# Values' products on four parts of 32 columns in place of two of 64, and the first pair turned and hashed whole

## The chip, the core and the metric

The kernel runs on one core of one Trainium2 chip. Five engines work side by side: TensorE (PE in the profile, its weight loads PEld), VectorE (DVE), ScalarE (ACT), GpSimd (POOL) and SyncE (SP), which here only issues DMAs. Each engine runs its own instructions in order and waits for others by semaphores. The metric is the device time of one execution, in microseconds.

## The reference

Attention over hash buckets, and behind it a feed-forward layer. Everything is float32.

```python
batch, n_heads, seq, head_dim = (4, 8, 768, 64)        # proj: 64 x 6
q_bits = (np.einsum('bhsd,dk->bhsk', q, proj) > 0)     # k_bits likewise
q_bucket = np.sum(q_bits * 2 ** np.arange(n_bits), axis=-1)
mask = q_bucket[:, :, :, None] == k_bucket[:, :, None, :]
scores = np.where(mask, np.matmul(q, k.transpose(0, 1, 3, 2)) / np.sqrt(D), -1000000000.0)
attn = np.exp(scores - np.max(scores, axis=-1, keepdims=True))
attn = attn / (np.sum(attn, axis=-1, keepdims=True) + 1e-09)
attn_out = np.matmul(attn, v)
x = attn_out.transpose(0, 2, 1, 3).reshape(3072, 512)
h = x @ w_in                                           # 512 x 2048
out = (h / (1.0 + np.exp(-1.702 * h))) @ w_out         # 2048 x 512
```

## The kernel before, in words

The attention stage takes two heads of one batch at a time: 16 pairs, `n` from 0 to 15. The two heads (index `j`) lie one above the other on the 128 partitions, 64 rows each, with the head's 64 dimensions as rows once keys and queries are turned. A sequence of 768 is six key tiles of 128 (`kt` or `t`), and two query halves of 384 columns (`c`, `HS` = 384).

Per pair TensorE does the following.

- `scores(n, c, kts)`, L426: for each key tile, two bf16 products that compare the hash bits (`kf`, `qf`) and two f32 products of keys and queries (`kT`, `qT`), one per head, into one PSUM tile `ps`. ScalarE takes the exponential of it into `es[c]` (L436). Three PSUM tiles of tag "s" take turns.
- `values(n, c, kts)`, L453: for each key tile and head the product of the head's values with the exponentials. The 64 value columns of a head are the weights, so the two heads' products write rows 0 to 63 and 64 to 127 of one PSUM tile `av`. A 385th column carries a tiny constant. `unload` (L474) lets ScalarE write the result to `xT`.
- `hashed(n)`, L405: four products, each with 32 weight columns, of projections with keys and queries; `featured` (L414) has VectorE make bits of them and DMAs bring the bits to `kf` and `qf`.
- `total(n)`, L480: four products, each with 32 weight columns of ones, which sum the exponentials (`dn`). VectorE inverts them (`invert`) and scales the result (`norm`, L507).

An f32 product is executed in two passes, each with a weight load of its own, so every f32 product stands in the profile as two loads and two matmuls.

GpSimd adds up the first three exponentials of a half (`add_low`, L443 and L444) and VectorE the rest (`add_high`, L449 and L451). VectorE also turns later pairs' keys and queries by 32 x 32 blocks (`turn`, L394) and converts one chunk of `w_in` per pair from float64, in which the weights come, to float32 (`convert`, L158).

For pairs 1 to 15 the order on TensorE is scores of half 0, scores of half 1, values of half 0, values of half 1, hash of pair n+2 (up to n = 13), sums of pair n. The order of instructions on TensorE, VectorE, ScalarE and GpSimd is that of the program text, since the schedule is set by hand for these four (`ORDERED`, L18). SP is not among them: its DMAs are placed by what they depend on. So a DMA that must not go early is held by a small VectorE memset of its destination, which stands at the right place in VectorE's order (`behind`, L315; `late`, L162).

The first pair has a path of its own, `first_pair`, L344. Keys and queries come in plain layout and are turned by TensorE with an identity (`turned`, L366: six f32 products for one half of one operand, moved out of PSUM by VectorE or ScalarE); `bits`, L374, hashes one half and makes its bits. Before the change, the first half of keys and of queries is turned and hashed ahead of the scores, then the second half of the keys is turned; the other three steps are returned as functions (`rest`) and called between the scores of the first pair (L534 to L543). The pair's values are fetched from inside `first_pair` (L364), behind a VectorE memset (L338).

The feed-forward stage follows on TensorE without a break: first products at L727 (a Strassen scheme of seven products with sums on VectorE and GpSimd), then second products at L839.

Of the kernel before, what the change touches and what calls it, by code (L numbers as in the profile page):

```python
# [38 lines left out]
def kernel(  # L39
# [17 lines left out]
    nc = tc.nc  # L57

    loader = [nc.sync]
    B, H, S, D = q.shape  # L60
# [3 lines left out]
    T = S // P  # L64
# [90 lines left out]
        later.append((m, x))  # L155
        masks[x] = m.to_broadcast([P, CW])

    def convert(cv, dst, src, queue=None, psum=None, late=False):  # L158


        raw = cv.tile([P, CW, 2], U32, tag="raw", name="raw")
        if late:  # L162
            nc.vector.memset(raw[:, 0, 0:1], 0)
        (queue or loader[0]).dma_start(out=raw, in_=src)

        def of(x):
            return x if len(dst.shape) == 2 else x.rearrange("p (x r) -> p x r", r=dst.shape[2])

        lo, hi = raw[:, :, 0], raw[:, :, 1]
        bits = cv.tile([P, CW], U32, tag="bits", name="bits")  # L170
        if psum is None:
            part, size = dst.bitcast(U32), hi.bitcast(F32)
        else:
            part = psum.tile([P, CW], U32, tag="part", name="part")
            size = psum.tile([P, CW], F32, tag="size", name="size")
        yield


        if psum is None:
            nc.vector.scalar_tensor_tensor(part, hi, 3, masks[0x3FFFFFFF], op0=Alu.logical_shift_left, op1=Alu.bitwise_and)  # L180
        else:
            nc.vector.tensor_scalar(part, hi, 3, 0x3FFFFFFF, op0=Alu.logical_shift_left, op1=Alu.bitwise_and)
        yield
        nc.vector.scalar_tensor_tensor(bits, hi, 0xC0000000, part, op0=Alu.bitwise_and, op1=Alu.bitwise_or)
        yield

        if psum is None:
            nc.vector.tensor_tensor(part, bits, masks[0xFF800000], op=Alu.bitwise_and)
        else:
            nc.vector.tensor_scalar(part, bits, 0xFF800000, None, op0=Alu.bitwise_and)  # L190

        nc.scalar.activation(size, hi.bitcast(F32), Act.Square)
        part = part.bitcast(F32)
        yield
        nc.vector.scalar_tensor_tensor(part, lo, 2.0**-52, part, op0=Alu.mult, op1=Alu.mult)
        yield
        nc.vector.tensor_tensor(dst, of(bits.bitcast(F32)), of(part), op=Alu.add)
        yield

        nc.vector.scalar_tensor_tensor(dst, of(size), (1.125 * 2.0**-15) ** 2, dst, op0=Alu.is_ge, op1=Alu.mult)  # L200
# [3 lines left out]
    in_chunks = [(w_in_sb[:, kc, f : f + CW], wi[kc, :, f : f + CW])  # L204
                 for f0 in range(0, FF // 2, CW) for f in (f0, FF // 2 + f0) for kc in range(KC)]
# [79 lines left out]
    def attention(ff):  # L285
# [4 lines left out]
        with actx:  # L290
            ld = actx.enter_context(tc.tile_pool(name="ld", bufs=1))
            wk = actx.enter_context(tc.tile_pool(name="wk", bufs=2))
            cv = actx.enter_context(tc.tile_pool(name="cv", bufs=1))
# [8 lines left out]
            es = [ep.tile([P, T, 2, HS + 1], F32, name=f"e{i}") for i in range(2)]  # L302
# [12 lines left out]
            def behind(x):  # L315

                nc.vector.memset(x, 0.0)
# [14 lines left out]
            def fetch_v(n):  # L332
                b, hp = pairs[n]
                x = ld.tile([P, T, 2, D], F32, tag="v", name="v", bufs=2)
                if n == 0:
                    x = x.rearrange("p t j d -> p (t j d)").rearrange("p (j t d) -> p t j d", j=2, d=D)
                vts[n] = x
                if n <= 1:  # L338
                    behind(x[:, 0, :, 0])
                for j in range(2):  # L340
                    order = "(t p) d -> p t d" if n else "(p t) d -> p t d"
                    loader[0].dma_start(out=x[:, :, j, :], in_=v[b, 2 * hp + j].rearrange(order, p=P))

            def first_pair():  # L344


                b, hp = pairs[0]
                x = {}
                for i, (name, src) in enumerate((("k", k), ("q", q))):
                    raw = raws[0, name] = ld.tile([P, S // 32, 32], F32, tag=name, name=name)  # L350
                    x[name] = raw.rearrange("p s i -> p (s i)").rearrange("p (j t d) -> p j t d", j=2, d=D)
                    for j, queue in enumerate((nc.sync, nc.scalar)):
                        queue.dma_start(out=x[name][:, j], in_=src[b, 2 * hp + j].rearrange("(p t) d -> p t d", p=P))
                    if i == 0:
                        for j, queue in enumerate((nc.sync, nc.scalar)):
                            queue.dma_start(out=pj[D * j : D * (j + 1)], in_=proj)
                    xts[0, name] = wk.tile([P, S], F32, tag=f"{name}T", name=f"{name}T")

                nc.scalar.activation(const.tile([1, 1], F32, name="first"), ones[0:1, 0:1], Act.Exp)
                for _ in range(4):  # L360
                    nc.tensor.matmul(aps.tile([P, 512], F32, tag="av", name="warm"), idle[:, 0:P], idle, start=True, stop=True)
                hash_weights()

                fetch_v(0)  # L364

                def turned(name, c, move):  # L366
                    tp = sps.tile([P, 2, 512], F32, tag="s", name="tp")[:, 0, 0:HS]
                    for i in range(GT):
                        for j in range(2):
                            nc.tensor.matmul(tp[D * j : D * (j + 1), i * P : (i + 1) * P], x[name][:, j, c * GT + i, :], ident,  # L370
                                             start=True, stop=True)
                    move(xts[0, name][:, c * HS : (c + 1) * HS], tp)

                def bits(name, c):  # L374
                    cols = slice(c * HS, (c + 1) * HS)
                    h = sps.tile([P, 2, 512], F32, tag="s", name="hash0")[:, 0, 0:HS]
                    nc.tensor.matmul(h, pf0[name].rearrange("p j d -> p (j d)"), xts[0, name][:, cols], start=True, stop=True)  # L377
                    nc.vector.tensor_scalar(feats[0][name][:, cols], h, above0[name][:, 0:1], FEAT[name],
                                            op0=Alu.is_gt, op1=Alu.mult)

                measure(0, "k")
                turned("k", 0, nc.vector.tensor_copy)
                turned("q", 0, nc.scalar.copy)
                measure(0, "q")
                bits("k", 0)
                bits("q", 0)
                turned("k", 1, nc.vector.tensor_copy)

                return (lambda: bits("k", 1), lambda: turned("q", 1, nc.vector.tensor_copy), lambda: bits("q", 1))

            def turn(n, name):
                x = raws[n, name]
# [3 lines left out]
            def measure(n, name):  # L396

                x = raws[n, name]
                i = 2 * n + "kq".index(name)
                junk = st.tile([P, S], BF16, tag="junk", name="junk", bufs=1)  # L400
                nc.scalar.activation(junk, x.rearrange("p s i -> p (s i)"), Act.Square, accum_out=sizes[:, i : i + 1])
# [51 lines left out]
            def values(n, c, kts):  # L453
                if 0 in kts:


                    if c and n == 0 or c and n + 2 > last:
                        avs[n, c] = mps.tile([P, HS + 1], F32, tag="m", name="av")
                    elif c:
                        avs[n, c] = sps.tile([P, 2, 512], F32, tag="s", name="av1")[:, 0, 0 : HS + 1]  # L460
                    else:
                        avs[n, c] = aps.tile([P, HS + 1], F32, tag="av", name="av")
                av, vt = avs[n, c], vts[n]
                for t in kts:
                    for j in range(2):
                        nc.tensor.matmul(av[D * j : D * (j + 1), :], vt[:, t, j, :], es[c][:, t, j, :],  # L466
                                         start=(t == 0), stop=(t == T - 1))

            def x_of(n):
                b, hp = pairs[n]  # L470
# [39 lines left out]
            conv = {}  # L510
# [4 lines left out]

            def begin(n):
                if 0 <= n - 2 < len(in_chunks) - LATE:
                    conv[n] = convert(cv, *in_chunks[n - 2], late=n == 2)
                    step(n)


# [10 lines left out]

            low, high, every = range(GT), range(GT, T), range(T)
            rest = first_pair()  # L534
            for x in "kq":
                fetch(1, x)
            scores(0, 0, low[:2])
            rest[0]()
            scores(0, 0, low[2:])
            rest[1]()  # L540
            add_low(0, 0)
            scores(0, 0, high)
            rest[2]()  # L543
            turn(1, "k")
            measure(1, "k")
            values(0, 0, low)
# [17 lines left out]
            for n in range(1, last + 1):  # L564
# [44 lines left out]
                if n < last:  # L609
                    begin(n + 1)  # L610
# [429 lines left out]
```

## Time and profile before

| what | value |
|---|---|
| runs before | 872.75 us median of 3 (872.38 to 874.32) |
| the profiled execution | 872.38 us, span 870.6 us |
| granted TensorE clock, mean | 0.997 |
| TensorE busy | 860.3 us, 99% of the span |
| VectorE, ScalarE, GpSimd busy | 719.4, 312.8, 313.3 us |
| attention on TensorE | up to 319.2 us, then first products to 607.7, second products to the end |
| one pair in the steady part | 19.14 us |
| values' products (L466) | 768 passes, 128.2 us busy |
| hash (L411) and sums (L487) | 15 and 16 blocks of eight passes |

In lines of the profile, "128*64 128x385" is a product with 128 rows and 64 columns of weights that writes or streams 385 columns. A row with "x48" merges 48 instructions: its first number is the start of the first, its second the busy time. Matmuls run on in a pipeline and their ends are modelled; starts are the better measure. The chain of work that ended last lists pieces of one engine's work, each with its share of the path. In a view by stretches, an engine's busy time stands with its instruction count in brackets, in the order TensorE, weight loads, VectorE, ScalarE, GpSimd, then the granted clock, the DMA share and GB/s.

### The profile page before, as it was taken

Reading aid. Unit: us, or ns where it says so; the run is one execution under the profiler, and the core shown is the slowest. Engines: PE = TensorE matmul, PEld = TensorE weight load, DVE = VectorE, ACT = ScalarE, POOL = GpSimd, SP = SyncE. Lnnn points to the kernel's source line nnn. Section 1 sums busy time; section 2 is a strip of 40 time slices with the busy share of each in tenths; the row PEclk is TensorE's granted clock in tenths of the full one; section 3 lists DMA queues with packets and bytes.
Section 4 is the critical chain, followed back from the end, with each engine's and each line's share of the span. In section 5 each row is a group of like instructions: output and inputs, shape, how many; then the busy total and the mean of one; then the engine's idle time right before and its main releaser. Section 6 shows DMA issues by size and latency. Waiting matters only on the chain.

```text
span 870.6 us, 11943 instructions
## 1 busy us (share of the span) xinstructions
PE 860.3 (99%) x4077; PEld 502.3 (58%) x4077; DVE 719.4 (83%) x1023; ACT 312.8 (36%) x518; POOL 313.3 (36%) x275
## 2 busy tenths in 40 slices
PE   9999999999999999999999999999999999999996
PEld 4444444444444444444444444444888888888885
DVE  4589999999999887778777778888888977897786
ACT  4866667777666643322233222332000000000000
POOL 4243223323323466665543344659903100000000
PEclk9999999999999999999999999999999999999998
DMA  4536654445763204555455555575844685468524
GB/s 103 92 56 128 108 90 84 84 85 111 108 95 68 61 3 171 189 208 198 174 195 181 206 181 204 183 253 179 299 164 157 199 245 198 162 212 242 193 97 99
DMA packets 169156, 132.00 MB, mean 152 GB/s; under 512 B 123616, under 2 KB 138112, under 8 KB 163712
## 3 DMA queue, kind: packets, MB, share of 16 engines
q1 hardware_dynamic: 166528, 129.70, 52.3%
q10 hardware_dynamic: 2560, 1.46, 0.7%
q8 instruction: 34, 0.56, 0.3%
q14 instruction: 34, 0.28, 0.1%
HBM read 79.69 MB, written 50.33 MB: 149 GB/s over the span
## 4 chain that ended last, share of the span: by engine, by line
PE 95%; DVE 3%; DMA 0%; issue 0%; SPq 0%; ACTq 0%; ACT 0%; DVEq 0%
PE product L727 33%; PE product L839 26%; PE ps L435 18%; PE av L466 15%; PE hash L411 1%; PE dn L487 1%; DVE y L819 1%; DVE xT L843 1%; DMA q<-in_q_dram 0%; PE hash L377 0%; DVE t_x L843 0%; PE tp L370 0%; DVE t2a L223 0%; DVE raw_g L222 0%; DVE v L843 0%
## 5 line engine op out<-in xcount | busy, mean ns | idle before, releaser
L436 ACT ACTIVATE e<-ps 128x768 f32<-128x768 f32 x192 | 151.2, 812 | 29.6 <-PE ps L435 27.0
L435 PE MATMUL ps<-qT,kT 64*128 64x384 f32 x768 | 155.1, 482 | 0.0
L727 PE MATMUL product<-xT,w_in_sb 128*128 128x512 f32 x288 | 135.5, 593 | 0.0
L466 PE MATMUL av<-e,v 128*64 128x385 f32 x768 | 128.2, 488 | 0.0
L443 POOL TENSOR_TENSOR acc<-e 128x768 f32<-128x768 f32 x32 | 51.1, 1597 | 196.8 <-ACT e L436 165.2
L735 ACT ACTIVATE c<-c 128x512 f32<-128x512 f32 x72 | 45.3, 630 | 186.8 <-issue 78.6
L466 PEld LDWEIGHTS av<-e,v 128*64 128x64 f32 x768 | 54.1, 136 | 71.6 <-issue 69.7
L727 PEld LDWEIGHTS product<-xT,w_in_sb 128*128 128x128 f32 x288 | 54.7, 190 | 69.0 <-issue 64.4
L727 PE MATMUL product<-t_x,s_in 128*128 128x512 f32 x192 | 90.2, 592 | 0.0
L435 PEld LDWEIGHTS ps<-qT,kT 64*128 64x128 f32 x768 | 68.0, 188 | 38.3 <-issue 38.2
L221 POOL TENSOR_TENSOR v<-c,u 128x512 f32<-128x512 f32 x24 | 34.2, 1423 | 122.4 <-ACT c L735 122.4
L852 ACT COPY u<-product 128x256 f32<-128x256 f32 x21 | 7.8, 372 | 172.1 <-PE product L839 138.9
L727 PEld LDWEIGHTS product<-t_x,s_in 128*128 128x128 f32 x192 | 36.5, 190 | 45.9 <-issue 43.2
L435 PE MATMUL ps<-qf,kf 64*128 64x384 bf16 x384 | 62.8, 324 | 0.0
L444 POOL TENSOR_TENSOR acc<-acc,e 128x768 f32<-128x768 f32 x32 | 56.4, 1763 | 2.7 <-ACT e L436 0.3
L449 DVE SCALAR_TENSOR_TENSOR acc<-e 128x768 f32<-128x768 f32 x32 | 46.0, 1438 | 4.0 <-ACT e L436 4.0
L727 PE MATMUL product<-xT,s_in 128*128 128x512 f32 x96 | 45.1, 592 | 0.0
L727 PE MATMUL product<-t_x,w_in_sb 128*128 128x512 f32 x96 | 45.1, 592 | 0.0
L435 PEld LDWEIGHTS <-kf 64*128 64x128 bf16 x384 | 18.9, 94 | 34.7 <-issue 5.7
L451 DVE TENSOR_TENSOR acc<-acc,e 128x768 f32<-128x768 f32 x32 | 35.6, 1112 | 3.7 <-DVE acc L449 0.5
L451 DVE TENSOR_TENSOR acc<-acc,acc 128x768 f32<-128x768 f32 x32 | 31.2, 974 | 6.7 <-POOL acc L444 3.1
L839 PE MATMUL product<-raw_g,xT 128*128 128x256 f32 x152 | 35.1, 379 | 0.0
(209 smaller groups left out, 1495.6 us busy)
## 6 DMA issues: line engine op xcount, KB each, us to landing
raw_g<-g_dram SPq DMA_DIRECT2D x22, 1024.0 KB
s_in<-g_dram SPq DMA_DIRECT2D x20, 1024.0 KB
g_dram<-c SPq DMA_DIRECT2D x72, 256.0 KB
g_dram<-t SPq DMA_DIRECT2D x48, 256.0 KB
raw<-in_moe_w_in_dram SPq DMA_DIRECT2D x16, 512.0 KB
raw<-in_moe_w_out_dram SPq DMA_DIRECT2D x16, 512.0 KB
v<-in_v_dram SPq DMA_DIRECT2D x32, 192.0 KB
g_dram<-u SPq DMA_DIRECT2D x24, 256.0 KB
```

Source lines behind the costliest of these rows:

```text
L221: return [lambda: eng.tensor_tensor(t1, b12, b11, op=Alu.subtract), lambda: eng.tensor_tensor(b12, b22, b12, op=Alu.subtract), lambda: eng ...
L411: nc.tensor.matmul(h[r0 : r0 + 32, :], pf[x], xts[n, x][:, c * HS : (c + 1) * HS], start=True, stop=True)
L435: nc.tensor.matmul(ps[:, j, 0:HS], a[hs, keys], m[hs, cols], start=not last, stop=last)
L436: nc.scalar.activation(es[c][:, kt, :, 0:HS], ps[:, :, 0:HS], Act.Exp, scale=1.0 / D**0.5)
L443: nc.gpsimd.tensor_tensor(acc, es[c][:, 0, :, 0:HS], es[c][:, 1, :, 0:HS], op=Alu.add)
L444: nc.gpsimd.tensor_tensor(acc, acc, es[c][:, 2, :, 0:HS], op=Alu.add)
L449: nc.vector.scalar_tensor_tensor(acc, e[0], T * TINY, e[1], op0=Alu.add, op1=Alu.add)
L451: nc.vector.tensor_tensor(acc, acc, x, op=Alu.add)
L466: nc.tensor.matmul(av[D * j : D * (j + 1), :], vt[:, t, j, :], es[c][:, t, j, :], start=(t == 0), stop=(t == T - 1))
L727: nc.tensor.matmul(ps, wq[LEFT[i]][:, kc, :], xq[RIGHT[i]][:, kc, :], start=(kc == 0), stop=(kc == K2 - 1))
L735: nc.scalar.activation(c, c, Act.Gelu_apprx_sigmoid)
L839: nc.tensor.matmul(ps, wq[LEFT[i]][:, c, :], gq[RIGHT[i]][:, c, :], start=(c == 0), stop=(c == F4 - 1))
```

## The change

There are two parts.

First, `values` splits the 64 value columns of each head into two parts of 32. Each key tile has four products of 32 weight columns (two per head, with the same exponentials streamed by both), in place of two of 64. They write the four quarters of the same PSUM tile `av`.

Second, the start of the first pair is put in another order. Both halves of the keys, then both halves of the queries are turned ahead of any hash. ScalarE moves both halves of the queries out of PSUM, VectorE both of the keys. Three of the four hashes are done ahead of the scores and the last one between the scores of key tiles 0 to 2 and 3 to 5. The pair's values are fetched after `first_pair`, without the memset that held them, so SP issues them directly behind the first queries. The memset that held the first chunk of `w_in` is gone as well (`late`): on SP that chunk's DMA now stands right behind the first pair's values, ahead of pair 1's keys and queries; before, it stood behind pair 3's bits.

```diff
-    def convert(cv, dst, src, queue=None, psum=None, late=False):
+    def convert(cv, dst, src, queue=None, psum=None):
...
-        if late:
-            nc.vector.memset(raw[:, 0, 0:1], 0)
         (queue or loader[0]).dma_start(out=raw, in_=src)
...
                 vts[n] = x
-                if n <= 1:
+                if n == 1:
                     behind(x[:, 0, :, 0])
...
                 hash_weights()
-                fetch_v(0)
...
                 measure(0, "k")
                 turned("k", 0, nc.vector.tensor_copy)
+                turned("k", 1, nc.vector.tensor_copy)
                 turned("q", 0, nc.scalar.copy)
+                turned("q", 1, nc.scalar.copy)
                 measure(0, "q")
                 bits("k", 0)
                 bits("q", 0)
-                turned("k", 1, nc.vector.tensor_copy)
-                return (lambda: bits("k", 1), lambda: turned("q", 1, nc.vector.tensor_copy), lambda: bits("q", 1))
+                bits("k", 1)
+                return lambda: bits("q", 1)
...
                     for j in range(2):
-                        nc.tensor.matmul(av[D * j : D * (j + 1), :], vt[:, t, j, :], es[c][:, t, j, :],
-                                         start=(t == 0), stop=(t == T - 1))
+                        for d in range(0, D, 32):
+                            nc.tensor.matmul(av[D * j + d : D * j + d + 32, :], vt[:, t, j, d : d + 32], es[c][:, t, j, :],
+                                             start=(t == 0), stop=(t == T - 1))
...
-                    conv[n] = convert(cv, *in_chunks[n - 2], late=n == 2)
+                    conv[n] = convert(cv, *in_chunks[n - 2])
...
             rest = first_pair()
+            fetch_v(0)
             for x in "kq":
                 fetch(1, x)
-            scores(0, 0, low[:2])
-            rest[0]()
-            scores(0, 0, low[2:])
-            rest[1]()
+            scores(0, 0, low)
+            rest()
             add_low(0, 0)
             scores(0, 0, high)
-            rest[2]()
```

## The prediction

> **What bounds the kernel now.** I read the page first (busy time per engine), then the chain that ended last around one pair of the attention stage, then TensorE and its weight loads at a seam between two kinds of products, then the first 20 us.
>
> ```profile
> PE 860.3 (99%) x4077; PEld 502.3 (58%) x4077; DVE 719.4 (83%) x1023; ACT 312.8 (36%) x518; POOL 313.3 (36%) x275
> PE 95%; DVE 3%; DMA 0%; issue 0%; SPq 0%; ACTq 0%; ACT 0%; DVEq 0%
> ```
>
> TensorE is busy for 99% of the span and 95% of the chain. So only what changes the length of TensorE's own sequence counts, and any change of it counts in full. The chain by pieces, two pairs of attention:
>
> ```profile
> 100.49 7.92 PE av L466 x48
> 108.41 0.78 PE hash L411 x8
> 109.19 0.65 PE dn L487 x8
> 109.84 9.80 PE ps L435 x72
> 119.63 7.92 PE av L466 x48
> 127.55 0.78 PE hash L411 x8
> 128.33 0.65 PE dn L487 x8
> ```
>
> A pair takes 19.14 us (119.63 less 100.49). The hash and the sums (dn) are the same work: four f32 products of 128 rows by 32 columns over 384 columns of data, each in two hardware passes, hence x8. But dn takes 0.65 and the hash before it 0.78. The reader is to see those 0.13 us: the hash follows the values' products, which lie on 64 columns, while dn follows products that already lie on 32. TensorE and its loads there:
>
> ```profile
> 126.41 1.15 PE L466 MATMUL av<-e,v 128*64 128x385 f32 x6
> 127.48 0.52 PE L411 MATMUL hash<-kT,pf_k 128*32 128x384 f32 x2
> 127.49 0.52 PE L411 MATMUL hash<-qT,pf_q 128*32 128x384 f32 x2
> 127.83 0.49 PE L411 MATMUL hash<-kT,pf_k 128*32 128x384 f32 x2
> 127.84 0.49 PE L411 MATMUL hash<-qT,pf_q 128*32 128x384 f32 x2
> 128.15 0.83 PE L487 MATMUL dn<-acc,ones 128*32 128x384 f32 x8
> ```
> ```profile
> 119.56 0.20 PEld L466 LDWEIGHTS av<-e,v 128*64 128x64 f32 x4 [0.54 <-issue]
> 119.94 0.14 PEld L466 LDWEIGHTS av<-e,v 128*64 128x64 f32 x2 [0.18 <-issue]
> 120.26 0.14 PEld L466 LDWEIGHTS av<-e,v 128*64 128x64 f32 x2 [0.18 <-issue]
> 120.59 0.14 PEld L466 LDWEIGHTS av<-e,v 128*64 128x64 f32 x2 [0.18 <-issue]
> 127.83 0.13 PEld L487 LDWEIGHTS dn<-acc,ones 128*32 128x32 f32 x4 [0.19 <-issue]
> ```
>
> In the values' block two products run side by side, and a new round of passes starts every 0.323 us (the loads at 119.94, 120.26, 120.59). In hash and dn four run side by side, all within 0.02 us of each other, and the round after starts 0.32 later (127.83 to 128.15). dn's weights were loaded at 127.83, during the hash: no gap at a seam of 32 to 32.
>
> **The change part by part.**
>
> *Rounds of the values.* 384 products of 64 columns become 768 of 32, so 768 passes become 1536. A key tile still needs two rounds, now of four. Cost per round by the nearest row: dn, two rounds in 0.65, against 24 rounds in 7.92 less the seam, 0.323. Zero, over 384 rounds. The cover is that all four columns' worth run at once; without it a key tile takes four rounds, 384 x 0.323 = 124 us more, and the hash and dn rows speak against that. Bounds: 0 below (the rounds stream the same 385 columns), and above 0.014 a round, because the starts of four parts are spread by 0.01 to 0.02 (127.48 to 127.49) and that spread might add up when rounds follow one another for 8 us, which no row shows. I take zero, as in dn. Issue: a round needs 8 instructions (4 loads, 4 passes) in 0.323, 40 ns each; the turning of keys at 8.97 issues 24 in 0.63, 26 ns each.
>
> The Trainium skill, in "TensorEngine Tiling (Array Packing)", Instruction Overhead, gives each matmul an overhead of about 60 cycles and so warns against splitting what is small. At the 2.4 GHz of "TensorE: Matmul & The Clock Gate" that is an estimate of 25 ns, and paid in line by 768 added passes 19 us; by that the forecast would be near 888. The dn rows show no such payment between four parts side by side, so the sum here does without it.
>
> *Seams.* After the values come the hash (14 times, at 24.19 and at 13 places from 50.92 to 280.6) or dn (the last two pairs). All 16 seams become 32 to 32 and lose 0.13: 16 x 0.13 = 2.1 us less. Also the first round of a values' block lasts 0.38 (119.56 to 119.94) against 0.35 in the hash (127.48 to 127.83), whose loads are shorter: 0.03 for each of 18 blocks (15 pairs with one, the first pair with three), 0.5 us less. Bounds: 0 (the waits below) and 2.6; I take 2.6, since both rows stand next to the place. Would something else hold the hash or dn then? The hash waits for VectorE's turns, which end at 121.5, 6 us ahead; dn waits for the acc that ends at 126.0, 2.1 us ahead. What is late next is VectorE itself, which looks full:
>
> ```profile
> 100.00:148.00 48.00, 48.00 (x340) 22.09 (x336) 45.61 (x57) 31.75 (x53) 16.12 (x10) 1.00 0.63 111
> ```
>
> 45.61 of 48 us. But its norm (L507) takes 1.96 there, overlapping a GpSimd sum that follows the exponentials and so TensorE, and takes 1.08 at 287.90. So 0.88 us a pair is give, and 0.16 is asked for.
>
> *The start.* Before and after do the same turns and hashes; their order differs.
>
> ```profile
> 3.68 1.64 PE L370 MATMUL tp<-ident,k 128*64 128x128 f32 x12
> 5.62 1.71 PE L370 MATMUL tp<-ident,q 128*64 128x128 f32 x12 [0.30 <-DMA q<-in_q_dram]
> 8.97 0.88 PE L370 MATMUL tp<-ident,k 128*64 128x128 f32 x12
> 11.54 0.91 PE L377 MATMUL hash<-kT,pf_k 128*128 128x384 f32 x2
> ```
>
> Before, scores begin at 9.82 and values at 17.48, with one hash, one turn and one hash between the six scores. After: keys' first turn from 3.65, and the second behind it (1.64 and 1.71 at the slow early pace, some 0.4 of it the last pass running out, so about 1.28 each in a sequence) until 6.2, which fills the 0.30 wait for the queries (landed 5.6). Queries' turns at 6.2 and 7.5, the second partly at the fast pace, until about 8.4. Three hashes of 0.65 from 8.5 to 10.5; the queries' bits are ready on VectorE at about 10.5 (hash done 9.9, 0.62 to write). Scores from 10.6: three at 0.81 to 13.0, the last hash with a seam on each side to 13.9, three more to 16.4. That is 1.1 us before 17.48. It has fewer seams, and nothing to wait for in the exponentials (ScalarE takes 0.81 each, three buffers).
>
> The values' load leaves its place behind VectorE's copy (5.98) and is issued at about 2.4, and the first chunk of w_in, which no VectorE memset holds any longer, goes right behind it on SP: 0.39 and 0.52 MB, beside the queries and ahead of pair 1's keys and queries. The chunk waits only for the first keys (3.6), so SP is not held for long. Worst case for the queries: all of the values ahead of them, 0.39 MB at the 250 GB/s that the busiest microseconds of the start moved at least (264 from 7 to 8 us, 301 from 4 to 5), 1.6 us, so turns from 7.2 rather than 6.2, and the gain falls to 0.1. For pair 1: keys and queries can be issued at about 6.3 and 9 where they were at 9.93 and 14.26, because their buffers come free sooner, and are wanted by VectorE at 18.12 and 21.98; 0.9 MB ahead costs 3.6 us at the same rate, so they land hardly later than before, and well before they are wanted. Bounds of the start: 1.3 gained (turns at the fast pace), 0.3 lost (queries late and slow pace longer). I take 0.8 gained, nearer the laid-out sequence than the worst case. The removed memsets (0.06 each on VectorE) count nothing; VectorE waits there 2.0 us for TensorE anyway.
>
> **Sum.** 2.6 + 0.8 = 3.4 us less. The profiled execution took 872.38 (span 870.6 and 1.8 around it), so 869.0; the median of the runs stands 0.37 above it, so 869.3. What follows attention is TensorE's chain without a gap (the product L727 takes 288.60 in one piece), so the gain is carried to the end.
>
> **The rivals.** (a) Longer rounds, the slower case: four parts in a long series cost more than two. 384 rounds; it turns the forecast at 3.4/384 = 9 ns a round. At the 14 ns above: 5.4 more, 874.7; at 20 ns 877. For it: no row has more than four such rounds in a series. Against: hash into dn keeps 0.32. (b) The start gains nothing or loses up to 0.3: 870.1 to 870.4. For it: 0.9 MB moved early beside the queries. Against: the second key turn covers the queries' wait. (c) The seams are saved but another engine holds the pair at 19.14 (VectorE's row above): only the start is left, 872.0. Against: the 0.88 us of give.
>
> **Numbers.** Forecast 0.56, (b) 0.14, (c) 0.13, (a) 0.17. A measurement of this kernel tells about 0.2%, 1.75 us, so faster is below 871.0 and slower above 874.5. Faster: forecast and nearly all of (b), 0.68. Same: (c) and the near end of (a), 0.16. Slower: 0.16. Range 867.6 (both terms at their best, 3.9, and the spread of the runs) to 873.6, which leaves out (a).
>
> **What would show it.** Right: av blocks near 7.9 with passes 128*32, the hash piece 0.65, a pair near 18.98, values first at about 16.4 to 16.9. Wrong: rounds above 0.33; the hash still 0.78; a wait before dn or scores on VectorE; values' first start after 17.5; queries landing after 6.5.

## The result, and the profile after

| | before | after |
|---|---|---|
| median | 872.67 us (six runs, 872.38 to 874.32) | 869.84 us (six runs, 869.47 to 871.11) |
| ratio of the times | | 0.9967, 95% interval 0.9954 to 0.9980 |
| the profiled execution | 872.38 us, span 870.6 | 869.86 us, span 868.1 |
| granted TensorE clock, mean | 0.997 | 0.996 |

The change is faster by 2.8 us by the medians and by 2.5 us by the two profiled executions. The forecast was 869.3. The page of the changed kernel, its busy times and its chain:

```profile
PE 857.6 (99%) x4845; PEld 499.7 (58%) x4845; DVE 719.2 (83%) x1020; ACT 313.4 (36%) x519; POOL 313.6 (36%) x275
PE 97%; DVE 2%; DMA 0%; issue 0%; ACTq 0%; ACT 0%; DVEq 0%
```

TensorE issues 768 passes more (4845 for 4077) and is busy 2.7 us less. So the split has not been paid for in rounds. The chain around one steady pair (start, length, what):

```profile
99.78 7.90 PE av L465 x96
107.68 0.65 PE hash L408 x8
108.33 0.65 PE dn L486 x8
108.97 9.79 PE ps L432 x72
118.77 7.90 PE av L465 x96
126.67 0.65 PE hash L408 x8
127.32 0.64 PE dn L486 x8
```

The pair takes 18.99 us (118.77 less 99.78). The hash has gone from 0.78 to 0.65, the values from 7.92 to 7.90 with twice the passes. TensorE at the seam (start, busy time, what):

```profile
118.70 7.97 PE L465 MATMUL av<-e,v 128*32 128x385 f32 x96
126.49 0.49 PE L408 MATMUL hash<-kT,pf_k 128*32 128x384 f32 x2
126.51 0.49 PE L408 MATMUL hash<-qT,pf_q 128*32 128x384 f32 x2
126.81 0.49 PE L408 MATMUL hash<-kT,pf_k 128*32 128x384 f32 x2
126.83 0.49 PE L408 MATMUL hash<-qT,pf_q 128*32 128x384 f32 x2
127.13 0.83 PE L486 MATMUL dn<-acc,ones 128*32 128x384 f32 x8
```

By starts, 24 rounds and the seam take 7.79 us (118.70 to 126.49), where before they took 7.92 (119.56 to 127.48). The weight loads of the same block:

```profile
118.70 0.16 PEld L465 LDWEIGHTS av<-e,v 128*32 128x32 f32 x8 [0.54 <-issue]
119.05 0.13 PEld L465 LDWEIGHTS av<-e,v 128*32 128x32 f32 x4 [0.19 <-issue]
119.37 0.13 PEld L465 LDWEIGHTS av<-e,v 128*32 128x32 f32 x4 [0.19 <-issue]
```

The first round lasts 0.35 (118.70 to 119.05), which was 0.38, and each one after it 0.32, with four loads where there were two. VectorE in the same stretch of 48 us as before (columns: TensorE, loads, VectorE, ScalarE, GpSimd, clock, DMA share, GB/s):

```profile
100.00:148.00 48.00, 48.00 (x490) 22.00 (x484) 45.59 (x57) 31.07 (x53) 16.06 (x10) 1.00 0.67 110
```

TensorE is still busy for all of it, so VectorE, at 45.59, does not hold the shorter pair. The start on TensorE (start, busy time, what, and in brackets the idle time before it):

```profile
4.04 2.90 PE L366 MATMUL tp<-ident,k 128*64 128x128 f32 x24 [0.32 <-DMA k<-in_k_dram]
6.64 2.61 PE L366 MATMUL tp<-ident,q 128*64 128x128 f32 x24
9.18 0.91 PE L373 MATMUL hash<-kT,pf_k 128*128 128x384 f32 x2
...
11.52 0.34 PE L432 MATMUL ps<-qf,kf 64*128 64x384 bf16 x2
...
17.42 2.15 PE L465 MATMUL av<-e,v 128*32 128x385 f32 x24
```

Here the change has brought next to nothing: the values begin at 17.42, and began at 17.48. The queries landed at 6.60 and 7.06 (5.58 and 5.75 before), their turns end at about 9.2, and the scores begin at 11.52.

An execution can be cut into three pieces by starts on TensorE: until the values first start, from there to the first product of the feed-forward layer, and the rest. This table, from the traces of all the kernels of this study, is the main tool of what follows; e1 to e11 are the experiments below.

| kernel | profiled execution | values first | from there to feed-forward | one steady pair | the rest |
|---|---|---|---|---|---|
| before | 872.38 | 17.48 | 301.74 | 19.140 | 553.16 |
| after | 869.86 | 17.42 | 299.29 | 18.990 | 553.15 |
| e1 split alone | 871.61 | 18.77 | 299.54 | 18.990 | 553.30 |
| e2 start alone | 871.08 | 16.14 | 301.74 | 19.140 | 553.20 |
| e3 64, then 32 | 873.92 | 18.84 | 301.85 | 19.140 | 553.23 |
| e4 32, then 64 | 874.43 | 17.40 | 303.82 | 19.278 | 553.21 |
| e5 after again | 870.33 | 17.84 | 299.29 | 18.990 | 553.20 |
| e6 loads held | 870.30 | 17.17 | 299.71 | 18.990 | 553.42 |
| e7 close warm-up | 869.82 | 17.20 | 299.29 | 18.990 | 553.33 |
| e8 close warm-up, loads held | 868.80 | 15.88 | 299.72 | 18.990 | 553.20 |
| e9 old order, close warm-up | 871.04 | 18.61 | 299.29 | 18.990 | 553.14 |
| e10 new order, close warm-up | 868.90 | 15.91 | 299.72 | 18.990 | 553.27 |
| e11 no warm-up | 869.71 | 17.19 | 299.29 | 18.990 | 553.23 |

The rest is the profiled execution's time less the values' first start and the piece behind it; it stays within 0.28 us over all thirteen. So nearly all that tells these executions apart lies in these two pieces. Between before and after, the attention stage gives 2.45 us and the start 0.06.

### The profile page after: what moved, and what is told of

It is laid out like the page before. It is cut to its first block, busy times and chain, and to the rows that moved or that the text cites. A ratio compares the mean times of both kernels' runs of the same rounds, so it can differ in the third digit from the quotient of the medians.

```text
span 868.1 us, 13473 instructions
## 1 busy us (share of the span) xinstructions
PE 857.6 (99%) x4845; PEld 499.7 (58%) x4845; DVE 719.2 (83%) x1020; ACT 313.4 (36%) x519; POOL 313.6 (36%) x275
## 4 chain that ended last, share of the span: by engine, by line
PE 97%; DVE 2%; DMA 0%; issue 0%; ACTq 0%; ACT 0%; DVEq 0%
PE product L724 33%; PE product L836 27%; PE ps L432 18%; PE av L465 15%; PE dn L486 1%; PE hash L408 1%; DVE xT L840 1%; PE tp L366 1%; DVE y L816 1%; DMA k<-in_k_dram 0%; PE hash L373 0%; DVE v L840 0%; DVE t2a L221 0%; DVE raw_g L220 0%; ACTq L823 0%
## 5 line engine op out<-in xcount | busy, mean ns | idle before, releaser
L465 PE MATMUL av<-e,v 128*32 128x385 f32 x1536 | 128.0, 487 | 0.0
L465 PEld LDWEIGHTS av<-e,v 128*32 128x32 f32 x1536 | 48.6, 109 | 76.2 <-issue 73.8
```

What stands on the lines that cost most here:

```text
L465: nc.tensor.matmul(av[D * j + d : D * j + d + 32, :], vt[:, t, j, d : d + 32], es[c][:, t, j, :], start=(t == 0), stop=(t == T - 1))
```

## The experiments

### The parts one at a time, and the seams: e1 to e4

The theory: the seams give their 2.5 us wherever the values stand at 32 columns next to hash or dn, and rounds of four parts cost nothing. The rival: the saving has another source (shorter passes, or the start). e1 is the kernel before with the split alone, e2 the changed kernel without the split, and e3 and e4 are the kernel before with one query half split:

```diff
                     for j in range(2):
-                        nc.tensor.matmul(av[D * j : D * (j + 1), :], vt[:, t, j, :], es[c][:, t, j, :],
-                                         start=(t == 0), stop=(t == T - 1))
+                        w = 32                       # e1;  e3: w = 32 if c else 64;  e4: w = 64 if c else 32
+                        for d in range(0, D, w):
+                            nc.tensor.matmul(av[D * j + d : D * j + d + w, :], vt[:, t, j, d : d + w], es[c][:, t, j, :],
+                                             start=(t == 0), stop=(t == T - 1))
```

> The kernel before with the split into four parts of 32 alone. My theory: all of what the pairs gain comes from the split, through the seams: values to the first product of the feed-forward stage 2.4 to 2.5 us shorter than before, a pair 19.00 in place of 19.14, the start as before (values first at 17.4 to 17.6). Time about 870.2, ratio 0.997. Rival (the reordered start and the early loads carry part of it): less than 1.5 us, over 871.

> The kernel after with the two products of 64 put back, so that only the order of the start and the early loads are new. My theory: a pair takes 19.14 again, hash 0.78; the start is worth what the profile after shows, 0.06 earlier, so the time is that of before within 0.5 us (872.2 to 873.2). Rival, the prediction's own term: 0.8 us less, 871.9. Rival, the early loads do harm later in the stage: over 873.5.

> The kernel before, with values of half 0 on two parts of 64 and of half 1 on four of 32. Seam theory: the change of width only moves from the end of the values to their middle, so values and hash together last as before within 0.05 (8.59 a pair from the first value to dn's start) and a pair 19.12 to 19.15; the hash itself 0.65. Rival, that rounds of 32 columns are themselves shorter or load better: half of the gain stays, a pair near 19.07.

> The kernel before, with values of half 0 on four parts of 32 and of half 1 on two of 64: as many products as the run beside it, in the other order, so one width change more (32 to 64 in the middle, 64 to 32 at the hash). Seam theory: a pair 0.10 to 0.15 longer than before, 19.24 to 19.29. Rival, rounds of 32 are shorter: a pair near 19.07, as in the run beside it.

Measured: e1 871.48 us (median of 12), ratio 0.9983 with the interval 0.9973 to 0.9993; e2 871.23 (of 11), 0.9984, 0.9975 to 0.9992; the kernel before beside them 873.18. e3 and e4 had one run each, 873.92 and 874.43. The chains around one pair, first of e2, in which the values stand on 64 columns:

```profile
99.15 7.92 PE av L463 x48
107.07 0.78 PE hash L408 x8
107.85 0.65 PE dn L484 x8
```

of e3, in which the half next to the hash stands on 32:

```profile
101.96 8.05 PE av L468 x72
110.01 0.65 PE hash L411 x8
110.66 0.65 PE dn L489 x8
```

and of e4, in which the half next to the hash stands on 64:

```profile
100.84 8.05 PE av L468 x72
108.90 0.78 PE hash L411 x8
109.68 0.65 PE dn L489 x8
```

This settles the seams. In e3 the hash is short (0.65), and the 0.13 stands inside the values instead (8.05 for 7.90), at the change from 64 to 32 between the halves: the pair takes 19.140, as before. e4 has two places where the width changes, in the values and ahead of the hash, and a pair of 19.278, 0.138 more. The number of passes is the same in e3 and e4. So what costs time is each change of the column width between products, 0.13 to 0.15 us, and not the width or the number of passes. Widths of 64 and 32 on 128 rows are all that was tried. e1 has the pair of the changed kernel, 18.990, without its start, and e2 the pair of the kernel before.

In time e1 and e2 missed what was expected of them: e1 was some 1.3 us slower, e2 some 1 to 2 us faster. In the profiled executions it is the start that came out otherwise. The stages give e1 2.20 us in attention, and the runs 1.70 (by the interval 0.6 to 2.4). Its profiled execution began its values at 18.77, 1.29 later than before's, although both have the same order of the start. e2's values began at 16.14, close to the 16.4 that the prediction had laid out, and with the fast pace from earlier on:

```profile
3.65 2.35 PE L366 MATMUL tp<-ident,k 128*64 128x128 f32 x24
6.05 0.88 PE L366 MATMUL tp<-ident,q 128*64 128x128 f32 x12
7.09 0.88 PE L366 MATMUL tp<-ident,q 128*64 128x128 f32 x12 [0.16 <-DVE kT L368]
...
16.14 1.19 PE L463 MATMUL av<-e,v 128*64 128x385 f32 x6
```

The changed kernel has the same instructions there and needs 2.61 for the 24 turns of the queries, where e2 needs 0.88 for twelve. So TensorE worked at half the pace for some time in the one execution and not in the other: a round of turns starts every 0.21 us at first and, from some moment on, every 0.107. The views print a granted clock of 1.00 for all of these stretches, but the trace's record of the clock has no entry for their first part: its first entry, full clock, stands at 7.74 in before, 8.42 in after, 10.09 in e1, 10.44 in e3, 7.39 in e4 and 5.27 in e2. There the same work becomes half as long, so the pace follows the granted clock, and ahead of the entry it is read from the length of the work. The mean clock in the tables counts the time ahead of the first entry as full and does not show it.

### What sets the start: e5 to e8

Two things were open: whether the early load of values and of the first chunk of w_in makes the queries late and costs the start, and what decides when TensorE's pace doubles. The theory: the pace follows the warm-up products, which start 0.64 us apart, each on a PSUM tile of its own; six on one tile, close together (0.43 apart in the traces of e7 and e8), would bring it forward. The rival: the time of the doubling varies from execution to execution. e5 is the changed kernel once more, e6 holds both loads back, e7 changes the warm-up, e8 does both:

```diff
-    def convert(cv, dst, src, queue=None, psum=None):
+    def convert(cv, dst, src, queue=None, psum=None, late=False):          # e6, e8
...
+        if late:
+            nc.vector.memset(raw[:, 0, 0:1], 0)
...
-                if n == 1:
+                if n <= 1:
                     behind(x[:, 0, :, 0])
...
-                for _ in range(4):                                          # e7, e8
-                    nc.tensor.matmul(aps.tile([P, 512], F32, tag="av", name="warm"), idle[:, 0:P], idle, start=True, stop=True)
+                warm = aps.tile([P, 512], F32, tag="av", name="warm")
+                for _ in range(6):
+                    nc.tensor.matmul(warm, idle[:, 0:P], idle, start=True, stop=True)
                 hash_weights()
+                fetch_v(0)                                                  # e6, e8
...
-                    conv[n] = convert(cv, *in_chunks[n - 2])
+                    conv[n] = convert(cv, *in_chunks[n - 2], late=n == 2)
...
             rest = first_pair()
-            fetch_v(0)
```

> The kernel after, once more, beside the next three. Theory from the first profiles: values first at 16.1 to 18.0, by when TensorE's pace doubles (turning rounds of 0.21 become 0.107; seen between 5.0 and 10 us, another time in every execution); from there to the feed-forward stage 299.3, as in the first profile. Median 2.5 to 3.5 us under that of before.

> The kernel after, with the memsets that hold the first values and the first w_in chunk put back, and the values fetched at their old place: only the loads are as before, the order of turns and hashes is new. Rival (early loads cost the start): queries land by 5.8 in place of 6.0 to 7.1, values first 0.4 to 0.8 earlier than in the kernel after at the same pace, 0.6 us less time. Theory (the pace decides, the loads hardly): within 0.5 us of the kernel after. The pair stays 18.99.

> The kernel after with six warm-up products of 512 columns on one PSUM tile, one right behind the other, in place of four with a wait between them. Pace theory: TensorE is busy without gaps from 1.2 us, the pace doubles by 5.0 us in every execution, values first at 16.0 to 16.6, median about 1 us under the kernel after and runs closer together. Rival (the pace comes at a random time whatever runs): values first between 16.1 and 18, no difference.

> Both: six close warm-up products and the loads held as before, with the split and the new order. If either the pace or the loads cost the start, this one begins earliest: values first at 15.8 to 16.4, 1.0 to 1.6 us under the kernel after. Rival: as the kernel after.

Measured, with the kernel before at 872.37 beside them (the moment at which the pace doubled is the first entry of the trace's clock record):

| kernel | median | ratio (interval) | queries landed | pace doubled | values first |
|---|---|---|---|---|---|
| e5 | 869.71 | 0.9963 (0.9949 to 0.9977) | 7.25, 7.44 | 8.87 | 17.84 |
| e6 | 869.77 | 0.9963 (0.9949 to 0.9976) | 5.92, 6.10 | 8.27 | 17.17 |
| e7 | 869.41 | 0.9966 (0.9954 to 0.9978) | 6.51, 7.46 | 5.92 | 17.20 |
| e8 | 869.10 | 0.9966 (0.9952 to 0.9979) | 5.70, 5.87 | 4.07 | 15.88 |

e5 came out as expected, and e6 within 0.5 us of it, as the theory had it. e7 missed: the pace doubled after 5.0, the values began at 17.20, and the median is 0.3 under e5's. e8 has the start that was expected, but only 0.6 of the 1.0 to 1.6 us.

The early loads do make the queries late: with them the queries' halves land at 6.5 to 7.5 in after, e5, e7 and e11 (e2 with 5.79 and 6.01 is the exception), and at 5.6 to 6.2 in before, e1, e6, e8, e9 and e10, where they are held. Yet e6 gains nothing by it in time. Its values begin 0.25 to 0.67 earlier than after's and e5's, but attention is 0.42 longer. How much the late queries cost depends on the pace. In e7, where it had doubled by 5.92, TensorE stops within the queries' turns,

```profile
7.51 1.52 PE L367 MATMUL tp<-ident,q 128*64 128x128 f32 x22 [0.52 <-DMA q<-in_q_dram]
```

and begins its values 1.32 after e8, which has the loads held and the pace at 4.07. In the changed kernel TensorE was still turning keys at the slow pace when the first half of the queries landed.

The place of e6's 0.42 is pair 1. VectorE there, of e6:

```profile
38.83 0.98 DVE L505 STREAM_TRANSPOSE rs<-r 128x768 f32<-128x768 f32 x1
40.35 1.57 DVE L510 TENSOR_TENSOR xT<-xT,rs 128x768 f32<-128x768 f32 x1 [0.54 <-ACT e L437]
```

and of the changed kernel:

```profile
39.08 0.98 DVE L501 STREAM_TRANSPOSE rs<-r 128x768 f32<-128x768 f32 x1
40.16 1.57 DVE L506 TENSOR_TENSOR xT<-xT,rs 128x768 f32<-128x768 f32 x1
```

In e6 the scaling of pair 0 starts 0.54 us after the transposition ahead of it ends, in the changed kernel 0.10. The 0.44 goes through VectorE's series into dn of pair 1. By the program text the scaling waits for VectorE and for the copy into xT on ScalarE; that copy had ended at 32.35. The profile names an exponential, and the times agree:

```profile
39.50 0.81 ACT L437 ACTIVATE e<-ps 128x768 f32<-128x768 f32 x1
```

It ends at 40.31, and the scaling starts 0.04 later; e8 and e10 have the same 0.54, and the same 0.04 behind an exponential. Why the scaling waits for an exponential in these three kernels is not shown. It is not the held loads by themselves: before, e1 and e9 hold them too, in the old order, and start the scaling about 0.11 after the transposition.

### The order alone, and no warm-up: e9 to e11

e8 had by far the earliest start. If the close warm-up is behind it, it should work in the old order too, and then the two orders can be compared at the same pace. e9 is e1 with the close warm-up, e10 is e8 again, and e11 leaves the warm-up out:

```diff
                 nc.scalar.activation(const.tile([1, 1], F32, name="first"), ones[0:1, 0:1], Act.Exp)
-                for _ in range(4):                                          # e11
-                    nc.tensor.matmul(aps.tile([P, 512], F32, tag="av", name="warm"), idle[:, 0:P], idle, start=True, stop=True)
                 hash_weights()
```

> The kernel before with the split and the six close warm-up products: old order of turns and hashes, loads held. It differs from the run with close warm-up and loads held in the order of the start alone, and the pace should have doubled by 5.8 us here too. Order theory (the prediction's start term: fewer seams, second key turn in the wait for the queries): values first at 16.6 to 17.1, 0.8 to 1.2 later than the 15.9 of the new order at the same pace, and 0.5 to 1.2 us more time than it. Rival (with the pace up early the order is worth nothing): values first by 16.2.

> The version with split, new order, loads held and six close warm-up products once more, beside the old order on the same chip: values first at 15.8 to 16.6 again (16.6 if the pace doubles as late as 5.8), median 868.8 to 869.6 where before is at 872.4, and under the old order beside it.

> The kernel after without any warm-up products before the first keys (TensorE idle until about 3.7 to 4.0). Pace theory (it doubles some time after TensorE has become busy): later than in the kernel after, at 8.5 to 12 us, values first at 17.8 to 18.8. Rival (it comes at a random time whatever runs): anywhere between 4 and 9, values first 16 to 17.8.

Measured, with the kernel before at 872.76: e9 869.71 (six runs, four from 869.63 to 869.74 and two at 871.00 and 871.04), ratio 0.9966, 0.9954 to 0.9979; e10 870.03 (seven runs, 868.90 to 870.84), 0.9971, 0.9960 to 0.9982; e11 869.71 (one run). e9's profile missed the expectation. Its start on TensorE:

```profile
4.12 1.63 PE L371 MATMUL tp<-ident,k 128*64 128x128 f32 x12 [0.20 <-DMA k<-in_k_dram]
6.11 1.70 PE L371 MATMUL tp<-ident,q 128*64 128x128 f32 x12 [0.36 <-DMA q<-in_q_dram]
7.75 1.65 PE L378 MATMUL hash<-kT,pf_k 128*128 128x384 f32 x2
```

Twelve turns in 1.63 and a hash in 1.65 are the slow pace, in spite of the close warm-up, until 9.54. The start of e10, with the same warm-up:

```profile
4.04 1.60 PE L371 MATMUL tp<-ident,k 128*64 128x128 f32 x24
6.04 1.70 PE L371 MATMUL tp<-ident,q 128*64 128x128 f32 x24 [0.40 <-DMA q<-in_q_dram]
...
15.91 2.15 PE L470 MATMUL av<-e,v 128*32 128x385 f32 x24
```

Here 24 turns take 1.60: the fast pace from 4.14 on. With the close warm-up the pace doubled at 4.07, 4.14, 5.92 and 9.54, with the spaced one at 5.27 to 10.44, without any at 8.15, earlier than the pace theory had expected of e11. The ranges overlap, so the rival stands: the moment varies from execution to execution, and whether a warm-up moves it on average stays open.

The traces do show what goes with the moment. In e2, e7, e8, e10 and e11 the timeline prints no wait of TensorE between its first product and the doubling, which came 2.9 to 4.7 us after that product. In the other eight TensorE waited in between, mostly for keys or queries, 0.30 (before) to 0.72 us (e1) in all, and the doubling came 6.2 to 9.3 us after the first product. No run changes these waits alone, so it is not shown that they are the cause, and the longer wait does not always go with the later doubling. All five executions in the old order have such a wait, three of the eight in the new.

The order alone can't be told from these times: e10's median lies 0.3 above e9's, inside both intervals, where it was expected below. No variant is measurably better than the changed kernel.

## Why the prediction was right, point by point

**Rounds of the values: right.** They cost nothing that can be measured in 384 rounds. The pair of 18.990, and a round of 0.32 with four parts, also rule out rival (a). The Trainium skill's Instruction Overhead ("TensorEngine Tiling (Array Packing)") of some 60 cycles a matmul does not show between parts that run side by side: 768 passes more cost no time that the profile shows.

**Seams and first rounds: right, 2.45 for 2.6.** A steady pair gives 0.150 (19.140 less 18.990), and e3 and e4 show that it hangs on the change of width. Two things in pair 1 were not foreseen. The hash of pair 2 stands there ahead of the values, so that a second seam, from hash to values, falls away: 0.669 for 0.782, 0.113 gained. And dn of pair 1 waits for VectorE, which takes back 0.116. VectorE in that place, and TensorE's loads of dn, both of the changed kernel:

```profile
37.19 0.56 DVE L492 STREAM_TRANSPOSE rt<-dn 128x384 f32<-128x384 f32 x1
...
50.15 0.96 DVE L448 TENSOR_TENSOR acc<-acc,acc 128x768 f32<-128x768 f32 x1
```
```profile
50.74 0.13 PEld L486 LDWEIGHTS dn<-acc,ones 128*32 128x32 f32 x2 [0.19 <-issue]
51.06 0.25 PEld L486 LDWEIGHTS dn<-acc,ones 128*32 128x32 f32 x6 [0.20 <-issue]
```

VectorE works from 37.19, when dn of pair 0 is there, to 51.11 with no wait for another engine, and the second half of dn starts 0.05 after that. "0.88 us a pair is give" was read from the steady pairs and holds there. In pair 1 there was none: rival (c) is true of that one pair, at 0.12 us. In e1 the series starts later still, since VectorE waits 3.00 us for pair 2's queries, and the loss is 0.25 more (299.54 for 299.29):

```profile
37.92 0.98 DVE L394 STREAM_TRANSPOSE qT<-q 128x768 f32<-128x768 f32 x1 [3.00 <-DMA q<-in_q_dram]
```

**The start: 0.06 for 0.8 in the two profiled executions, and its size not settled.** The step that failed there is "keys' first turn from 3.65" and, behind it, "Queries' turns at 6.2 and 7.5, the second partly at the fast pace, until about 8.4". It laid the new order over the landings and the pace of the one execution that was shown. In the changed kernel the turns of the keys start at 4.04, after a wait of 0.32 for the keys, and the queries' turns at 6.64; these run at the slow pace until 8.42 (7.74 in before) and end at about 9.2. The queries did land 1.0 to 1.3 us later, not far from the prediction's worst case of 1.6, and its sign ("queries landing after 6.5") came true, but keys were being turned until 6.64, and the queries' weight loads waited only 0.2 for the landing. The late keys need not be the early loads' doing: with the loads held the first turn started between 3.68 (before) and 4.13 (e6).

Landing and pace vary. For the same order the values first started from 17.40 to 18.84 (old: before, e1, e3, e4, e9) and from 15.88 to 17.84 (new). Each spread is wider than the term. That the new start is worth something is shown by e2, whose seams are those of before and whose interval is 0.7 to 2.2 us below the kernel before (0.9992 and 0.9975 of 873.18). The changed kernel against e1, which lacks only the second part of the change, points the same way: ratios of 0.9967 and 0.9983, 1.4 us, though their intervals overlap. The size stays open: read between executions whose pace doubled at like times, it is by an estimate 0.5 to 0.6 (old order 17.48 at 7.74 and 18.61 at 9.54, so 17.7 to 17.9 between 8.15 and 8.42; new order 17.2 to 17.4 there), and e9 against e10, which loses 0.43 again in pair 1, shows none.

**The sum.** 2.45 and 0.06 make the 2.5 of the profiled executions. By the medians the gain is 2.8, and the forecast stood 0.5 below the measured median: 0.15 of the seams and about 0.7 of the start were not found in the profiled executions, and the medians give 0.3 of it back. Since executions of one kernel differ at the start by more than the start's term, that the forecast came within 0.5 is in part luck.

The Trainium skill, in "TensorE: Matmul & The Clock Gate", Part 1, tells of a clock that starts at half rate and is raised after a busy window of about 3.4 us whose phase differs from run to run, and puts the ramp at under 1% of a span. The rows agree on the halves (a round of turns every 0.21 and every 0.107 us), on the variation and on the size: all starts, of both orders, lie from 15.9 to 18.8, 2.9 us or 0.33% of the span. Without a wait of TensorE the doubling came 2.9 to 4.7 us after the first product, near the page's window; with waits it came up to 9.3 us after it, later than one window.

## What to carry to other kernels

Where TensorE is the bound, look at the seams: blocks of products with different column widths (64 and 32 here) cost 0.13 to 0.15 us at each change, and a block that is split into parts of its neighbours' width keeps its own length as long as the parts fill the columns side by side. Judge slack of another engine in each stage where the gain is wanted, the first pairs too, and not by a steady stretch alone. A change at the start of a kernel should be weighed against several profiles of the same kernel, since the start of one execution may differ from the next by more than the change is worth; a cut of the execution at fixed points (here three pieces) separates the two. And a granted clock of 1.00 in a view should be compared with the length of equal work, since it is also printed where the trace has no record.

## What was not expected of the hardware

- The cost of a change of column width also falls between two blocks of the same kind of product (8.05 for 7.90 us in e3 and e4), and it arises from 32 to 64 as from 64 to 32 (e4's extra 0.138 us a pair).
- TensorE starts at half of its later pace, and the moment at which it doubles ran from 4.07 to 10.44 us over the thirteen executions. It came 2.9 to 4.7 us after the first product where TensorE did not wait in between, and 6.2 to 9.3 where it did.
- Transfers started early beside the first queries delayed their landing by about 1 us in four of five profiled executions (6.5 to 7.5 for 5.6 to 6.2), and in the new order holding them back gained no time that shows, since pair 1 then lost 0.42 us on VectorE (e6).
